# Column steps run one pair ahead with half blocks of gw2 between them, and x's normal form made a second time on GpSimd

## The chip, the cores and the metric

The kernel runs on one core of a Trainium2 chip. The metric is the time of the whole program on the device in microseconds (us); smaller is better. The profile names the engines PE (TensorE, matrix products), PEld (its weight loads), DVE (VectorE), ACT (ScalarE), POOL (GpSimd) and SP (SyncE, which here only issues transfers).

## The reference

One block of a network, forward and backward, in one program. With x of 2048 tokens and 448 channels, and LN a layer norm without weights:

```
h   = x + irfft2( rfft2(LN(x)) * (w_r + i w_i) )
u   = gelu( LN(h)^T w1 + b1 )            # mixes the 2048 tokens into 1792
out = h + ( u w2 + b2 )^T
```

The outputs are `out` and the gradients of x, w_r, w_i, w1, b1, w2 and b2 for a given gradient of `out`; inputs and outputs are bf16. `out_1` is the gradient of x, `out_2` and `out_3` those of w_r and w_i, `out_4` that of w1 (2048x1792), `out_6` that of w2 (1792x2048).

## The kernel before

Tokens lie on the 128 partitions in 16 tiles (`NT`), channels along the row. The program runs in stages, and a scheduler puts the instructions of each engine in one fixed order when the program is built; each engine's queue, and each queue of transfers, is then worked through in that order. `tc.issue_after` and `tc.high_priority` steer it.

1. **Rows forward.** `load_x` brings x in four groups of four tiles. `Norm.stats` and `Norm.finish` make mean and deviation of each group (`nb` is -mean/deviation) and the normal form `xln`; `fft_rows` transforms the rows of a group. Products `dg(j)` of the gradient with w2 (14 of them, 16 matmuls each, L535) fill TensorE meanwhile. Their weights `w2T` come by transposing transfers on SP's queue into a ring of four buffers.
2. **Columns forward.** `fft_cols` makes 9 column steps for r = 0, 8, 1, ..., 7. In a step, `part` runs 8 small matmuls into one or two PSUM tiles, ACT copies one of them (`gi`), DVE adds and subtracts (`gg`), and `out_r` runs three matmuls with `gg` and lets ACT copy the result to `dst`. `cmul` multiplies by the complex filter in six groups of r, `ifft_cols` goes back.
3. SP's queue is a hand-made chain (`nxt`). Behind the tables it holds four stores of `xln` to DRAM (`xln_d`, 448 KB each), then more of `w2T`, `xs_d` (a copy of the spectrum) and `w1c`, the weights of stage 4.
4. **Rows back, MLP forward, and du.** `rows_mid`/`rows_out`, the second norm, gelu (L622), the second product (L691) and `du` times w1 (L748).
5. **Backward block.** The gradient `dh` goes through the same `fft_rows`, `fft_cols`, `cmul` and `ifft_cols` (here with `twice=True`), then `rows_mid_twice` and `rows_out` for each of 16 tiles h. Between them lie the big products: `gw2(j)`, j = 0 to 13, a block of four PSUM tiles of 128x512 (L224: full matmuls, L231: the last 64 rows, two at a time) that four copies empty and one store writes to `out_6`; and `gw1(h)`, 16 blocks, for `out_4`. `outer` issues a block: the full matmuls of its first two tiles, the 64-row ends of all four, the full ones of the last two. Blocks 1 to 5 of `gw2` stand after the column steps in the text, with lower priority, and the scheduler draws their matmuls forward into TensorE's gaps; blocks 6 to 13 follow with h = 0 to 7, then `gw1` with h = 8 to 15, and the last eight blocks of `gw1` in pairs. In the row loop, `norm_back` needs the normal form of x again: `xr`, four tiles at a time in a ring of two buffers, loaded from `xln_d` on POOL's queue. From h = 10 on, `grad_w` makes one of six groups of the gradients of w_r and w_i on DVE from `xs_b`, which is loaded from `xs_d` at h = 7 into the slot that `goT` leaves after the last `gw2`.

Of the kernel before, what the change touches and what calls it, by code (L numbers as in the profile page):

```python
# [135 lines left out]
def kernel(  # L136
# [78 lines left out]
        with tc.issue_after(behind.ins):  # L215
            ld(t[0:64, 3, :], t[64:128, 3, :])

    def outer(first, second, lhs, rhs, shared=True):


        def full(outs, opens):
            for ps, a, b in outs:
                for c in range(3):
                    last = pe.matmul(ps, lhsT=lhs[:, c, a], rhs=rhs[:, c, b],  # L224
                                     start=opens and c == 0, stop=not opens and c == 2)
            return last

        def tails(outs, opens):
            for i, (ps, a, b) in enumerate(outs):
                k = slice(64 * (i % 2), 64 * (i % 2) + 64)  # L230
                last = pe.matmul(ps, lhsT=lhs[k, 3, a], rhs=rhs[k, 3, b], start=opens, stop=not opens)  # L231
            return last

        last = full(first, True)
        with tc.high_priority() if shared else nullcontext(), tc.issue_after(last.ins):
            tails(first, False)
            last = tails(second, True)
        with tc.issue_after(last.ins):
            return full(second, False)

    def ev(out, in_, on):
        if on == "a":
# [62 lines left out]
    gb1 = consts.tile([P, NFB], F32, name="gb1")  # L305
    gb2 = consts.tile([P, NT], F32, name="gb2")

    xln_d = dram.tile([P, NT, D], BF16, name="xln_d")
    xs_d = dram.tile([P, 2, XW], BF16, name="xs_d")
    hn_d = dram.tile([S, D], BF16, name="hn_d")  # L310
    hln_d = dram.tile([NT, P, D], BF16, name="hln_d")
# [4 lines left out]
    class Norm:  # L316
        def __init__(self, src, dst, rstd, eps_col, scale, nm):
            self.src, self.dst, self.rstd, self.eps_col, self.scale, self.nm = src, dst, rstd, eps_col, scale, nm

        def stats(self, h):  # L320
            if h % 4 == 0:
# [8 lines left out]
        def finish(self, g):  # L330
            mv = self.mv[:, :].rearrange("p (i c) -> p i c", c=2)
            r = self.rstd[:, 4 * g:4 * g + 4]
            sq = col(4, f"sq_{self.nm}")
            ac.activation(out=sq[:], in_=mv[:, :, 1], func=ACT.Sqrt, bias=self.eps_col[:], scale=self.scale)
            ve.reciprocal(out=r, in_=sq[:])
            nb = col(4, f"nb_{self.nm}")
            ve.scalar_tensor_tensor(out=nb[:], in0=mv[:, :, 0], scalar=-1.0, in1=r, op0=ALU.mult, op1=ALU.mult)
            for i in range(4):
                h = 4 * g + i

                if (i > 1 or g == 3) if self.nm == "x" else (i > 1 and g == 3):
                    ve.tensor_scalar(out=self.dst[:, h, :], in0=self.src[:, h, :], scalar1=self.rstd[:, h:h + 1],
                                     scalar2=nb[:, i:i + 1], op0=ALU.mult, op1=ALU.add)
                else:
                    ac.activation(out=self.dst[:, h, :], in_=self.src[:, h, :], func=ACT.Identity,  # L345
                                  scale=self.rstd[:, h:h + 1], bias=nb[:, i:i + 1])
# [30 lines left out]
            done = ev(zt[:, :, :, 8 * h:8 * h + 8], pz[:, :, :].rearrange("p c (s k) -> p c s k", k=8), on[i])  # L377
        return last, done

    def fft_cols(zt, dtab, dst, second=None, twice=False):  # L380
        w = 226 if twice else DF

        def part(out, r, odd, s=0):

            if twice:
                for c, chunk in enumerate((3, 2) if odd else (0, 1)):
                    o = 113 * ((2 + 2 * s if odd else 0) + c)
                    pe.matmul(out[:, 113 * c:113 * c + 113], lhsT=zt[:, chunk, r, :], rhs=dtab[:, o:o + 113],
                              start=True, stop=True)
                return  # L390
            for c in range(2):
                o = DF * (2 + 2 * c + s if odd else c)
                pe.matmul(out, lhsT=zt[:, 2 * odd + c, r, :], rhs=dtab[:, o:o + DF], start=(c == 0), stop=(c == 1))

        def sums(nm):
            gg = k1([P, 2, w], nm)
            return gg, gg[:].rearrange("p a (k c) -> p a c k", c=2) if twice else gg[:]

        def by_k(ps):
            return ps[:].rearrange("p a (c k) -> p a c k", c=2) if twice else ps[:]  # L400

        def out_r(r, gg):
            px = ps_sp([P, 2, DF])
            k, i = R_ORDER.index(r) // 8, R_ORDER.index(r) % 8
            pe.matmul(px[:, :, :], lhsT=hf[:, k, 0, i, :], rhs=gg[:, :, 0:DF], start=True, stop=False)  # L405
            pe.matmul(px[:, 0, :], lhsT=hf[:, k, 1, i, :], rhs=gg[:, 1, 0:DF], start=False, stop=False)
            pe.matmul(px[:, 1, :], lhsT=hf[:, k, 2, i, :], rhs=gg[:, 0, 0:DF], start=False, stop=True)
            ac.copy(out=dst[:, :, r * DF:(r + 1) * DF], in_=px[:])

        for r in (0, 8, 1, 2, 3, 4, 5, 6, 7):  # L410
            pr = ps_sp([P, 2, w])
            part(pr[:, 0, :], r, 0)
            part(pr[:, 1, :], r, 1, 0)
            if r in (0, 8):
                gg, out = sums("gg")
                ac.copy(out=out, in_=by_k(pr))
                out_r(r, gg)
                continue
            pi = ps_sp([P, 2, w])
            part(pi[:, 0, :], 16 - r, 1, 1)  # L420
            part(pi[:, 1, :], 16 - r, 0)
            gi = f2([P, 2, w], "gi")
            ac.copy(out=gi[:], in_=pi[:])  # L423
            for rr, op in ((r, ALU.add), (16 - r, ALU.subtract)):
                gg, out = sums("gg")
                last = ve.tensor_tensor(out=out, in0=by_k(pr), in1=by_k(gi), op=op)  # L426
                out_r(rr, gg)
            if r == 2 and second is not None:
                second(last)


    R_GROUPS = ((0, 3), (14, 16), (3, 6), (11, 14), (6, 8), (8, 11))
# [14 lines left out]
                done(r0, r1, last)  # L447


    def ifft_cols(ys, ab, twice=False):  # L450
        lasts = []

        def half(r):
# [14 lines left out]
        for r in (1, 2, 3, 4, 5, 6, 7, 0, 8):  # L468
            p0 = half(r)
            if r in (0, 8):  # L470
                for kind in range(2):
                    ev(ab[:, kind, :, :, r, :], view(p0)[:, kind], "av"[kind])
                continue
            p1 = half(16 - r)
            t1 = f2([P, 2, 2, P], "t1")
            ac.copy(out=t1[:], in_=p1[:])
            st_ = 16 - 2 * r
            ve.tensor_tensor(out=ab[:, 0, :, :, r:17 - r:st_, :].rearrange("p c h k l -> p k c h l"),
                             in0=view(p0), in1=view(t1), op=ALU.add)
            ve.tensor_tensor(out=ab[:, 1, :, :, 16 - r:r - 1:-st_, :].rearrange(  # L480
                "p c h k l -> p k c h l"), in0=view(p0), in1=view(t1), op=ALU.subtract)
# [68 lines left out]
    di0 = table([P, 4 * DF], "di0", "di")  # L550
    kinv = table([P, 3, P], "kinv")
    ident = table([P, P], "ident")
    for g in range(4):
        nxt(ld, xln_d[:, 4 * g:4 * g + 4, :], xln[:, 4 * g:4 * g + 4, :])
    with tc.issue_after(folded[3][1].ins):
        neg(hf[:, 0, 2], hf[:, 0, 1])
    xs = slot(3, [P, 2, XW], "xs")
# [36 lines left out]
    for j in range(4, NFB):  # L594
        dg(j)
        if j == 6:
            nxt(ld, xs_d[:], xs[:])
        if j in (5, 9, 13):
            load_w1c(nxt)


# [155 lines left out]
        load_w(w_b[:, :, 0:XW], lambda load, out, in_: load(out, in_))  # L757
    fft_rows(dh, zt2, 2, "aava", None, True)

    first = []  # L760

    def gw2(j, on):
        s6 = w4([P, S], "s6")
        pws = [ps_mm([P, 512]) for n in range(4)]
        outs = [(pws[n][:], slice(j * P, (j + 1) * P), slice(512 * n, 512 * n + 512)) for n in range(4)]
        mm = outer(outs[:2], outs[2:], g_t, goT)
        for n in range(4):
            ev(s6[:, 512 * n:512 * n + 512], pws[n][:], on[n])
        first.append(mm)
        return st(out_6[j * P:(j + 1) * P, :], s6[:])  # L770

    gw2(0, "aaaa")
    fft_rows(dh, zt2, 3, "aava", first[0], True)
    ds = slot(3, [P, 2, XW], "ds")
    fft_cols(zt2, df0, ds, None, True)
    cmul(lambda r0, r1: (w_b[:, 0, r0 * DF:r1 * DF], w_b[:, 1, r0 * DF:r1 * DF]), ds, w_b, True)
    ab2 = slot(7, [P, 2, 2, NT, NR, 8], "ab2")
    ifft_cols(w_b, ab2, True)

    def small_out(dst, src, n):  # L780
        sb = consts.tile([P, n], BF16, name=f"sb{n}")
# [14 lines left out]
    ld_t4(du_t[:], du_d[:])  # L796
    ld_twice(hlnT, w1T_last)
    ld_twice(du_t, w1T_last)
    xs_b = slot(4, [P, 2, XW], "xs_b")

    def gw1(h, ps):
        s4 = w4([P, F], "s4")
# [14 lines left out]

    def gw1_four(h):
        outs, out = gw1(h, ps_mm)
        outer(outs[:2], outs[2:], hlnT, du_t)  # L820
        out()


    def grad_w(group):
# [11 lines left out]

    for j in range(1, 6):
        gw2(j, "aaaa")  # L840
    mids = [rows_mid_twice(ab2, di1, h) for h in range(2)]
    for h in range(NT):
        if h + 2 < NT:
            mids.append(rows_mid_twice(ab2, di1, h + 2))
        if h % 4 == 0:
            xr = ring.tile([P, 4, D], BF16, tag="xr", bufs=2, name="xr")
            ld(xr[:], xln_d[:, h:h + 4, :], po)
        with tc.issue_after(mids[-1][1].ins):
            py = rows_out(mids[h][0])
        gx = k1([P, D], "gx")  # L850
        norm_back(py, False, xr[:, h % 4, :], rstd_x[:, h:h + 1], -1.0 / D, dh[:, h, :], gx[:])
        st(rows(out_1[0])[:, h, :], gx[:])
        if h < 8:
            gw2(h + 6, "aaav")
        else:
            gw1_four(h - 8)
        if h == 7:
            ld(xs_b[:], xs_d[:])
        if h > 9:
            grad_w(R_GROUPS[h - 10])  # L860

    for h in range(8, NT, 2):
        outs, out = gw1(h, ps_mm)
        outs_2, out_2nd = gw1(h + 1, ps_sp)
        outer(outs, outs_2, hlnT, du_t, False)
# [32 lines left out]
```

## Time and profile before

| | us |
|---|---|
| median of 3 runs (360.67 to 362.02) | 361.34 |
| the profiled execution | 361.35 |
| its span from first to last instruction | 359.5 |

The 1.85 us between the last two lie around the span. The profile page gives busy times by engine and by slices of the span; other views of the same trace list who waited for whom, the chain of work that ended last, the instructions in order of time, and busy time in chosen stretches. A matmul's row is longer than the time that it holds the engine, since matmuls are pipelined and their ends modelled. The granted TensorE clock was 0.997 of full speed over the span.

### The profile page before, as it was taken

The numbers are of one execution on the slowest core, as the hardware profiler recorded it, in microseconds if no ns is written. First come the engines' busy times: TensorE is split into PE (matmuls) and PEld (weight loads), VectorE is DVE, ScalarE is ACT, GpSimd is POOL, SyncE is SP. The second block draws the span as 40 slices with busy tenths as digits, with TensorE's granted clock in tenths as the row PEclk, the third lists the DMA queues.
The fourth block names the chain that finished last, engine by engine and source line by source line (L and its number), as shares of the span: only waits on it lengthen the run. The fifth ranks groups of instructions, "written<-read, shape, count | busy, mean of one in ns | idle before, by whom it ended". The sixth has DMA issues, their size and how long they took to land.

```text
span 359.5 us, 5818 instructions
## 1 busy us (share of the span) xinstructions
PE 334.7 (93%) x2100; PEld 184.9 (51%) x2115; DVE 243.9 (68%) x580; ACT 210.5 (59%) x429; POOL 58.1 (16%) x106
## 2 busy tenths in 40 slices
PE   0799996999999999999999999989999999999994
PEld 0456664666664555555555555544555545454442
DVE  4883776967773999822226887837799997599600
ACT  2574653446658999304703344678766666677573
POOL 1000010001113011330160000010100243335620
PEclk9999999999999999999999999999999999999998
DMA  8999999999699999999999888599293365956664
GB/s 280 265 230 335 241 282 279 283 259 299 206 332 263 320 330 261 319 354 312 214 241 217 173 181 164 201 213 200 89 250 99 142 234 188 352 195 249 239 255 154
DMA packets 132988, 87.18 MB, mean 243 GB/s; under 512 B 92032, under 2 KB 124032, under 8 KB 132576
## 3 DMA queue, kind: packets, MB, share of 16 engines
q1 hardware_dynamic: 124768, 56.48, 65.8%
q0 software_dynamic: 8048, 30.31, 23.4%
q8 instruction: 16, 0.26, 0.3%
q14 instruction: 12, 0.10, 0.1%
q10 hardware_dynamic: 144, 0.03, 0.0%
HBM read 32.52 MB, written 30.76 MB: 176 GB/s over the span
## 4 chain that ended last, share of the span: by engine, by line
PE 71%; DVE 12%; ACT 7%; DMA 7%; issue 2%; ACTq 0%; DVEq 0%
PE ps_mm L224 13%; PE ps_mm L748 12%; PE ps_mm L622 6%; PE ps_sp L691 6%; PE ps_mm L691 6%; DMA w2T<-in_B_w_dram 6%; PE ps_mm L535 6%; PE ps_sp L622 5%; PE ps_mm L231 3%; PE ps_sp L224 2%; ACT s L243 2%; DVE bs_x L324 1%; PE ps_sp L405 1%; ACT zt L243 1%; PE ps_sp L376 1%
## 5 line engine op out<-in xcount | busy, mean ns | idle before, releaser
L243 ACT CAST s<-ps_mm 128x512 bf16<-128x512 f32 x96 | 48.4, 568 | 20.1 <-PE ps_mm L231 13.1
L535 PE MATMUL ps_mm<-go_nat,w2T 128*128 128x448 bf16 x224 | 50.9, 361 | 4.1 <-DMA w2T<-in_B_w_dram 4.1
L748 PE MATMUL ps_mm<-du,w1T 128*128 128x449 bf16 x224 | 43.4, 353 | 0.0
L224 PE MATMUL ps_mm<-goT,g_t 128*128 128x512 bf16 x158 | 41.2, 379 | 0.6 <-issue 0.3
L691 PEld LDWEIGHTS <-w2c 128*128 128x128 bf16 x224 | 21.9, 98 | 20.5
L748 PEld LDWEIGHTS <-w1T 128*128 128x128 bf16 x224 | 21.7, 97 | 20.7
L622 PEld LDWEIGHTS <-w1c 128*128 128x128 bf16 x224 | 21.8, 98 | 19.9 <-issue 1.0
L535 PEld LDWEIGHTS <-w2T 128*128 128x128 bf16 x224 | 21.8, 99 | 20.0 <-DMA w2T<-in_B_w_dram 5.4
L691 PE MATMUL ps_sp<-gT,w2c 128*128 128x448 bf16 x112 | 30.3, 352 | 0.0
L691 PE MATMUL ps_mm<-gT,w2c 128*128 128x448 bf16 x112 | 30.3, 352 | 0.0
L224 PE MATMUL ps_mm<-du_t,hlnT 128*128 128x512 bf16 (+1 forms) x141 | 30.1, 352 | 0.3 <-issue 0.2
L224 PEld LDWEIGHTS <-hlnT 128*128 128x128 bf16 x192 | 17.8, 98 | 20.5 <-issue 5.1
L426 DVE TENSOR_TENSOR gg<-ps_sp,gi 128x450 bf16<-128x450 f32 (+1 forms) x28 | 16.6, 642 | 16.8 <-ACT gi L423 16.8
L194 POOL DMA_DIRECT2D out_dram<-s x29 | 15.6, 538 | 62.6 <-ACT s L243 51.3
L622 PE MATMUL ps_mm<-hln,w1c 128*128 128x448 bf16 x112 | 23.8, 352 | 0.3 <-ACT hln L345 0.3
L712 ACT ACTIVATE nm<-ps_mm,rstd_h 128x1 f32<-128x1 f32 x16 | 4.2, 262 | 33.8 <-PE ps_mm L748 33.8
L224 PEld LDWEIGHTS <-g_t 128*128 128x128 bf16 x168 | 15.1, 97 | 15.5 <-issue 3.9
L622 PE MATMUL ps_sp<-hln,w1c 128*128 128x448 bf16 x112 | 22.8, 352 | 0.0
L696 DVE SCALAR_TENSOR_TENSOR h<-ps_mm,b2col,hr 128x448 bf16<-128x448 f32 x8 | 5.1, 680 | 25.8 <-PE ps_mm L691 25.8
L703 ACT ACTIVATE junk<-go_r 128x448 bf16<-128x448 bf16 x16 | 9.2, 576 | 18.4 <-DMA go_r<-in_grad_out_dram 18.0
L243 ACT CAST zt<-ps_sp 128x512 bf16<-128x512 f32 x26 | 13.4, 596 | 6.9 <-PE ps_sp L376 6.9
L578 DVE TENSOR_TENSOR x<-ps_sp,x 128x448 bf16<-128x448 f32 x16 | 10.0, 625 | 9.5 <-PE ps_sp L515 8.6
(157 smaller groups left out, 661.5 us busy)
## 6 DMA issues: line engine op xcount, KB each, us to landing
w1c<-in_B_w_dram SPq DMA_DIRECT2D x7, 1024.0 KB, 7.0
w2c<-in_B_w_dram SPq DMA_DIRECT2D x8, 896.0 KB, 12.4
out_dram<-s POOLq DMA_DIRECT2D x14, 512.0 KB, 3.0
out_dram<-s POOLq DMA_DIRECT2D x15, 448.0 KB, 3.0
xs_d<-xs SPq DMA_DIRECT2D x1, 1800.0 KB, 7.4
xs_b<-xs_d SPq DMA_DIRECT2D x1, 1800.0 KB, 9.9
x<-in_A_x_dram SPq DMA_DIRECT2D x4, 448.0 KB, 4.3
go_nat<-in_grad_out_dram SPq DMA_DIRECT2D x2, 896.0 KB, 7.3
```

Source lines behind the costliest of these rows:

```text
L194: return (eng or po).dma_start(out=out, in_=in_)
L224: last = pe.matmul(ps, lhsT=lhs[:, c, a], rhs=rhs[:, c, b], start=opens and c == 0, stop=not opens and c == 2)
L231: last = pe.matmul(ps, lhsT=lhs[k, 3, a], rhs=rhs[k, 3, b], start=opens, stop=not opens)
L243: return ac.copy(out=out, in_=in_)
L426: last = ve.tensor_tensor(out=out, in0=by_k(pr), in1=by_k(gi), op=op)
L535: pe.matmul(pg[:], lhsT=w2T[j][:, t, :], rhs=go_nat[:, t, :], start=(t == 0), stop=(t == NT - 1))
L578: ve.tensor_tensor(out=hn[:, h, :], in0=py[:], in1=x[:, h, :], op=ALU.add)
L622: pe.matmul(pu[:], lhsT=wc[:, h, o:o + P], rhs=hln[:, h, :], start=(h == 0), stop=(h == NT - 1))
L691: pe.matmul(p2[i][:], lhsT=w2c[t0 // 4][:, j, i * P:(i + 1) * P], rhs=gT[:, j, :], start=(j == 0), stop=(j == NFB - 1))
L696: ve.scalar_tensor_tensor(out=h2[:], in0=p2[i][:], scalar=b2col[:, t:t + 1], in1=hr[:, i, :], op0=ALU.add, op1=ALU.add)
L703: ac.activation(out=junk[:], in_=go_r[:, h, :], func=ACT.Copy, accum_out=gb2[:, h:h + 1])
L748: w1_last = pe.matmul(pd[:], lhsT=w1T[:, j, :], rhs=du[:, j, 0:D + 1], start=(j == 0), stop=(j == NFB - 1))
```

## The change

Three things change. (1) `outer` becomes the generator `halves`, which stops after each half block; the blocks of `gw2` from 1 and of `gw1` stand in one queue, `blocks()`, and `fill(n)` takes n halves from it: one or two in each backward column step, one at r = 1, 3, 5 of the backward `ifft_cols`, two (one block) in each step of the row loop. In the backward column steps `out_r` of one pair of r is issued behind `part` of the next pair. In the row loop `gw2` so ends at h = 5 and not 7, `xs_b` is loaded at h = 5, `grad_w` runs at h = 8 to 13, ten blocks of `gw1` lie in the loop and six behind it. (2) The four stores of `xln_d` are gone. `xr` is loaded from x itself, again on POOL's queue, and GpSimd makes the normal form of each tile in place with one `tensor_scalar` (16 in all); `nb` is kept in a tile of its own. (3) The loads of `w1c` stand behind `dg(7)`, `dg(10)` and `dg(13)`, not 5, 9 and 13.

In the order that the scheduler makes of it, POOL's queue issues the first two loads of `xr` right behind the two small loads of `b1r` and `b2r` at the start, since nothing holds them any more, and the first eight `tensor_scalar` stand behind them; the other eight lie between the stores of the row loop. The ninth `w2T` (for `dg(8)`) stands on SP's queue right behind the tables, followed by two more, `xs_d`, another `w2T`, and then the first `w1c`.

```
-    def outer(first, second, lhs, rhs, shared=True):
+    def halves(first, second, lhs, rhs, shared=True):
...
             tails(first, False)
             last = tails(second, True)
+        yield last
         with tc.issue_after(last.ins):
-            return full(second, False)
+            last = full(second, False)
+        yield last
+
+    def outer(*args):
+        return list(halves(*args))[-1]
...
-    xln_d = dram.tile([P, NT, D], BF16, name="xln_d")
...
+            self.nb = consts.tile([P, NT], F32, name=f"nb_{nm}")
...
-    def fft_cols(zt, dtab, dst, second=None, twice=False):
+    def fft_cols(zt, dtab, dst, second=None, twice=False, fill=None):
...
+        waiting = []
         for r in (0, 8, 1, 2, 3, 4, 5, 6, 7):
             pr = ps_sp([P, 2, w])
             part(pr[:, 0, :], r, 0)
             part(pr[:, 1, :], r, 1, 0)
+            done = []
             if r in (0, 8):
                 gg, out = sums("gg")
                 ac.copy(out=out, in_=by_k(pr))
-                out_r(r, gg)
-                continue
...
+                done.append((r, gg))
+            else:
+                pi = ps_sp([P, 2, w])
+                part(pi[:, 0, :], 16 - r, 1, 1)
+                part(pi[:, 1, :], 16 - r, 0)
+                gi = f2([P, 2, w], "gi")
+                ac.copy(out=gi[:], in_=pi[:])
+                for rr, op in ((r, ALU.add), (16 - r, ALU.subtract)):
+                    gg, out = sums("gg")
+                    last = ve.tensor_tensor(out=out, in0=by_k(pr), in1=by_k(gi), op=op)
+                    done.append((rr, gg))
...
+            waiting += done
+            if not fill or r:
+                for rr, gg in waiting if not fill else waiting[:-len(done)]:
+                    out_r(rr, gg)
+                waiting = done if fill else []
+                if fill:
+                    fill(2 if r in (3, 6) else 1)
+        for rr, gg in waiting:
+            out_r(rr, gg)
...
             p1 = half(16 - r)
+            if fill and r in (1, 3, 5):
+                fill(1)
...
-    for g in range(4):
-        nxt(ld, xln_d[:, 4 * g:4 * g + 4, :], xln[:, 4 * g:4 * g + 4, :])
...
-        if j in (5, 9, 13):
+        if j in (7, 10, 13):
             load_w1c(nxt)
...
-        mm = outer(outs[:2], outs[2:], g_t, goT)
-        for n in range(4):
-            ev(s6[:, 512 * n:512 * n + 512], pws[n][:], on[n])
...
+        for i, mm in enumerate(halves(outs[:2], outs[2:], g_t, goT)):
+            for n in (2 * i, 2 * i + 1):
+                ev(s6[:, 512 * n:512 * n + 512], pws[n][:], on[n])
+            if i:
+                st(out_6[j * P:(j + 1) * P, :], s6[:])
+            yield mm
...
+    def blocks():
+        for j in range(1, NFB):
+            yield from gw2(j, "aaaa" if j < 7 else "aaav")
+        for h in range(NT):
+            yield from gw1_four(h)
+
+    others = blocks()
+
+    def fill(n):
+        return [next(others) for i in range(n)]
+
     ds = slot(3, [P, 2, XW], "ds")
-    fft_cols(zt2, df0, ds, None, True)
+    fill(1)
+    fft_cols(zt2, df0, ds, None, True, fill)
...
-    ifft_cols(w_b, ab2, True)
+    ifft_cols(w_b, ab2, True, fill)
...
-    for j in range(1, 6):
-        gw2(j, "aaaa")
...
-            ld(xr[:], xln_d[:, h:h + 4, :], po)
+            ld(xr[:], rows(A_x[0])[:, h:h + 4, :], po)
+
+            for i in range(h, h + 4):
+                po.tensor_scalar(out=xr[:, i - h, :], in0=xr[:, i - h, :], scalar1=rstd_x[:, i:i + 1],
+                                 scalar2=nx.nb[:, i:i + 1], op0=ALU.mult, op1=ALU.add)
...
-        if h < 8:
-            gw2(h + 6, "aaav")
-        else:
-            gw1_four(h - 8)
-        if h == 7:
+        fill(2)
+        if h == 5:
+            xs_b = slot(4, [P, 2, XW], "xs_b")
             ld(xs_b[:], xs_d[:])
-        if h > 9:
-            grad_w(R_GROUPS[h - 10])
-
-    for h in range(8, NT, 2):
+        if 8 <= h < 14:
+            grad_w(R_GROUPS[h - 8])
+
+    for h in range(10, NT, 2):
```

More of the change, by code (lines that the diff above doesn't have):

```diff
@@ L335, in finish @@
             ve.reciprocal(out=r, in_=sq[:])
-            nb = col(4, f"nb_{self.nm}")
-            ve.scalar_tensor_tensor(out=nb[:], in0=mv[:, :, 0], scalar=-1.0, in1=r, op0=ALU.mult, op1=ALU.mult)
+            nb = self.nb[:, 4 * g:4 * g + 4]
+            ve.scalar_tensor_tensor(out=nb, in0=mv[:, :, 0], scalar=-1.0, in1=r, op0=ALU.mult, op1=ALU.mult)
             for i in range(4):
@@ L416, in fft_cols @@
                 ac.copy(out=out, in_=by_k(pr))
-                out_r(r, gg)
-                continue
[L419 to L429, printed above, removed]
+                done.append((r, gg))
[9 more added lines that the diff above has]
+                    done.append((rr, gg))
+                if r == 2 and second is not None:
+                    second(last)
+            waiting += done
[7 more added lines that the diff above has]
+            out_r(rr, gg)
     R_GROUPS = ((0, 3), (14, 16), (3, 6), (11, 14), (6, 8), (8, 11))
@@ L447, in cmul, with ifft_cols @@
                 done(r0, r1, last)
-    def ifft_cols(ys, ab, twice=False):
+    def ifft_cols(ys, ab, twice=False, fill=None):
         lasts = []
@@ L758 @@
     fft_rows(dh, zt2, 2, "aava", None, True)
-    first = []
     def gw2(j, on):
@@ L765, in gw2 @@
         outs = [(pws[n][:], slice(j * P, (j + 1) * P), slice(512 * n, 512 * n + 512)) for n in range(4)]
-        mm = outer(outs[:2], outs[2:], g_t, goT)
-        for n in range(4):
-            ev(s6[:, 512 * n:512 * n + 512], pws[n][:], on[n])
[L769 to L773, printed above, removed]
+        for i, mm in enumerate(halves(outs[:2], outs[2:], g_t, goT)):
[4 more added lines that the diff above has]
+            yield mm
+    first = list(gw2(0, "aaaa"))
+    fft_rows(dh, zt2, 3, "aava", first[-1], True)
+    def blocks():
[6 more added lines that the diff above has]
+        return [next(others) for i in range(n)]
     ds = slot(3, [P, 2, XW], "ds")
-    fft_cols(zt2, df0, ds, None, True)
+    fill(1)
+    fft_cols(zt2, df0, ds, None, True, fill)
     cmul(lambda r0, r1: (w_b[:, 0, r0 * DF:r1 * DF], w_b[:, 1, r0 * DF:r1 * DF]), ds, w_b, True)
     ab2 = slot(7, [P, 2, 2, NT, NR, 8], "ab2")
-    ifft_cols(w_b, ab2, True)
+    ifft_cols(w_b, ab2, True, fill)
     def small_out(dst, src, n):
@@ L798 @@
     ld_twice(du_t, w1T_last)
-    xs_b = slot(4, [P, 2, XW], "xs_b")
     def gw1(h, ps):
@@ L819, in gw1_four @@
         outs, out = gw1(h, ps_mm)
-        outer(outs[:2], outs[2:], hlnT, du_t)
-        out()
+        for i, mm in enumerate(halves(outs[:2], outs[2:], hlnT, du_t)):
+            if i:
+                out()
+            yield mm
     def grad_w(group):
```

## The prediction

> **What bounds the kernel now.** The page first, then TensorE's waits over the whole run, then the chain that ended last.
>
> ```profile
> span 359.5 us, 5818 instructions
> PE 334.7 (93%) x2100; PEld 184.9 (51%) x2115; DVE 243.9 (68%) x580; ACT 210.5 (59%) x429; POOL 58.1 (16%) x106
> DMA  8999999999699999999999888599293365956664
> ```
>
> TensorE is busy for 93% of the span, so a change can only win idle time of TensorE or its late start and end. The transfer engines are nearly full in the first 27 of 40 slices, up to some 240 us. So a transfer that is moved into that part pushes others back.
>
> ```profile
> PE ps_sp L376 <- DVE eo L370: 10.9, 1, 10.9
> PE ps_mm L535 <- DMA w2T<-in_B_w_dram: 4.1, 2, 3.5
> PE ps_sp L405 <- DVE gg L426: 1.2, 5, 0.4
> PE ps_sp L405 <- ACT gg L416: 0.5, 1, 0.5
> ...
> 47.45 11.25 DMA w2T<-in_B_w_dram
> ...
> 289.98 1.29 PE ps_mm L224 x6
> ...
> 352.93 2.24 ACT s L243 x5
> ```
>
> The first four lines are waits (total us, times, longest), the others stand in the chain (start, us, what). TensorE starts at 10.9, when the first rows are ready. It then stands still once for long, 3.5 us before `dg(8)`, because its weights `w2T` come late, and 0.6 us before `dg(11)`. In the backward column steps it waits for `gg` of DVE and ACT, 1.7 us as shown. At the end nothing is hidden: the last copies take 2.24 us and their stores the rest. Six matmuls of 512 columns take 1.29 us, 0.215 each.
>
> **The change part by part.** The sum is made against the profiled execution: 361.35 us, span 359.5 and 1.85 around it. It is 0.01 off the median of the runs shown, 361.34.
>
> *The start.* The loads of `xr` wait for nothing now, and two of them move to the head of POOL's queue.
>
> ```profile
> 0.74 0.39 SPq L191 DMA_DIRECT2D x<-in_A_x_dram  x1
> ...
> 1.92 0.54 POOL L191 DMA_DIRECT2D b2r<-in_B_b_dram  x1
> 2.27 0.71 SPq L191 DMA_DIRECT2D go_nat<-in_grad_out_dram  x1
> ...
> 3.02 7.61 SPq L197 DMA_TRANSPOSE w2T<-in_B_w_dram  x1
> ...
> 8.73 0.62 DVE L324 BATCH_NORM_STATS2 bs_x<-x 128x6 f32<-128x448 bf16 x1
> ...
> 10.69 1.04 SPq L191 DMA_DIRECT2D x<-in_A_x_dram  x2
> ...
> 10.88 1.89 PE L376 MATMUL ps_sp<-kf,eo 128*128 128x128 bf16 x16 [10.88 <-DVE eo L370]
> ...
> 12.74 1.68 PE L535 MATMUL ps_mm<-go_nat,w2T 128*128 128x448 bf16 x4
> ...
> 5.00:10.00 5.00, 0.00 (x0) 0.00 (x0) 4.36 (x14) 1.71 (x3) 0.00 (x0) 1.00 1.13 379
> 10.00:15.00 5.00, 4.12 (x23) 2.56 (x24) 3.87 (x15) 3.04 (x7) 0.00 (x0) 1.00 1.08 268
> ...
> go_nat<-in_grad_out_dram SPq DMA_DIRECT2D x2, 896.0 KB, 7.3
> xln_d<-xln SPq DMA_DIRECT2D x4, 448.0 KB, 8.4
> xr<-xln_d POOLq DMA_DIRECT2D x4, 448.0 KB, 5.8
> ```
>
> SP's queue issues x, go_nat, x, go_nat and then the first `w2T`, whose row ends at 10.63 and holds up the next loads of x until 10.69. I read that as: it waits until the loads ahead have landed. POOL would issue its two loads from 2.5 us on (1.92 + 0.54), when only the first x is about done. They are 2 x 448 KB, 0.92 MB, and the stretch from 5 to 10 us moves 379 GB/s at a full share (1.13): 2.4 us of transfer ahead of everything that is still queued. Second group of x: 896 KB before 10.63, so landed at about 8.2, used by DVE at 8.73 in front of `eo`. It would land at 10.6, so DVE and the first matmul are 1.9 later; `w2T`, and `dg(0)` at 12.74, 2.4 later. I take +2.1. Bounds: 0, if POOL's loads only fill gaps, and 3.4, at the 268 GB/s of the stretch behind.
>
> The Trainium skill, "Trainium Kernel Development and Optimization", section Key Constraints, says that transfers from the SP, ACT and POOL queues run on the same 16 engines and interleave, which speaks against this part of the change; that the share exceeds 1 here fits it.
>
> *The wait for w2T.* The four stores of `xln`, 1.8 MB, stood ahead of the ninth `w2T`, and the early `xr` loads from them ran beside it.
>
> ```profile
> SPq L197 <- DMA hi<-tab_hi: 1.8, 1, 1.8
> ...
> L191 SPq DMA_DIRECT2D xln_d<-xln x4: 366/540/1040, 42.8 to 44.6; - x4
> ...
> 78.88 0.74 PE ps_mm L535 x3
> ...
> 95.03 1.05 PE ps_mm L622 x5
> ...
> w1c<-in_B_w_dram SPq DMA_DIRECT2D x7, 1024.0 KB, 7.0
> ...
> ident<-tab_ident SPq DMA_DIRECT2D x1, 32.0 KB, 7.7
> ...
> 56.68 0.69 DVE L247 TENSOR_SCALAR hi<-hi 128x2048 bf16<-128x2048 bf16 x1
> ...
> 58.74 0.55 PE L535 MATMUL ps_mm<-go_nat,w2T 128*128 128x448 bf16 x2 [3.54 <-DMA w2T<-in_B_w_dram]
> ```
>
> In the new order that `w2T` stands where the first store stood, right behind the tables; it no longer waits for `hi`. Before, it was issued at 47.45 and landed 11.25 later. Issued where the first store was, at 42.8, behind `ident` (landed 7.7 after an issue just before that, so by 50), and given the 4 to 5 us that are left of the 11.25 without the stores, it lands at about 54, or 56 with the late start. `dg(8)` wants it at 55.2 (58.74 less 3.54), or 57.3 with the late start. So the wait goes: 3.54 shown, and 0.16 more, because a 512-column matmul's row is 0.378 long where the next starts after 0.215. What is late next is DVE, busy to 57.4 (56.68 + 0.69) with the filter, which TensorE's pause had hidden: up to 0.8. I take -3.4, between -3.7 and -2.9. The 0.6 before `dg(11)` goes too: the first two loads of `w1c`, 2 MB, no longer stand ahead of `xs_d` and that `w2T` (bounds 0 and -0.8). Moving `w1c` costs nothing as long as it lands before L622 starts, at 95; it now stands behind the `w2T` that `dg(11)` uses at 78.9. If it were late, `dg(12)` would wait for it first.
>
> *GpSimd's 16 pieces.* No row shows such an operation on GpSimd. The nearest are the same operation on DVE and ACT:
>
> ```profile
> L342 DVE TENSOR_SCALAR xln<-x,rstd_x,nb_x x10: 379/392/398, 8.1 to 24.6; 128x448 bf16<-128x448 bf16 x10
> L345 ACT ACTIVATE xln<-x,nb_x,rstd_x x6: 744/754/760, 8.1 to 21.4; 128x448 bf16<-128x448 bf16 x6
> ```
>
> 0.39 to 0.75, and I take 0.75, the slower engine's. Queued behind them are stores on POOL, which have no reader but the ring of four buffers. They delay nobody unless they slow DVE (a rival, below). For that I put +0.2 at the start.
>
> *Column steps.* The half blocks now fill what DVE and ACT leave.
>
> ```profile
> 236.00:264.00 28.00, 25.82 (x198) 13.71 (x200) 17.52 (x31) 23.47 (x46) 2.67 (x5) 1.00 0.82 176
> 264.00:282.00 18.00, 17.50 (x132) 11.24 (x132) 16.60 (x35) 11.34 (x24) 1.07 (x2) 1.00 0.60 157
> 282.00:335.00 53.00, 52.35 (x332) 25.38 (x337) 45.90 (x112) 35.80 (x78) 20.27 (x38) 1.00 0.62 229
> ...
> L224 PE MATMUL ps_mm<-goT,g_t 128*128 128x512 bf16 x49 | 13.0, 378 | 0.2 <-issue 0.2
> L243 ACT CAST s<-ps_mm 128x512 bf16<-128x512 f32 x19 | 10.7, 595 | 2.5 <-PE ps_mm L231 2.2
> ...
> L405 PE MATMUL ps_sp<-gg,hf 128*128 128x450 bf16 x16 | 5.7, 354 | 1.7 <-DVE gg L426 1.0 <-ACT gg L416 0.5
> ...
> DVE t_r L441 <- DMA xs_b<-xs_d: 3.2, 1, 3.2
> ```
>
> (Stretches: length, then busy PE, PEld, DVE, ACT, POOL, clock, DMA; then groups of 236 to 264.) In the steps from 236 to 264 TensorE waits for DVE's `gg` 1.0 shown, four times, each 0.16 more: 1.6. A pair of lead covers that, since DVE then has a half block (6 x 0.215) and the other pair's `out_r` to finish. The wait for ACT at r = 0 and 8 stays. But ACT is at 23.5 of 28, and the new order puts about one block more into this stage: four copies of 0.595, 2.4, so 25.9 in 26.4. `gi` then stands behind copies. And `ifft_cols` behind it (264 to 282) has DVE at 16.6 of 18, whatever TensorE does. I take -0.9, bounds -1.6 and +0.6 (one copy late on the chain).
>
> *The row loop.* TensorE's work is the same, 52.35 of 53. `xs_b` comes two steps earlier, and so does DVE's 3.2 wait for it; five and not three groups of `grad_w` stand ahead of the last `eo`. Cover: `rows_mid_twice` runs two steps ahead, and DVE has 53 - 45.9 - 3.2 = 3.9 left. The last eight pieces of GpSimd fall here. I take +0.2, bounds 0 and 3.0 (four pieces of 0.75 where DVE is full). The end is the same, three pairs of `gw1` and not four.
>
> Sum: +2.1 - 3.4 - 0.6 + 0.2 - 0.9 + 0.2 = -2.4, so 361.35 - 2.4 = 359.0 us. A measurement can tell about 0.5% from no change: 1.8 us, below 359.5 or above 363.2.
>
> **The rivals.** *The start costs nothing.* POOL's loads run in gaps, or land after the second x. For it: the slice before 5 us is not full. Against: the share of 1.13 from 5 on. Then 359.0 - 2.1 = 356.9.
>
> *Slower: GpSimd and DVE block each other.* If a piece on GpSimd holds up a DVE operation with two inputs in memory for its length, the four `eo` operations of the first two groups, on the chain to the first matmuls, lose up to 4 x 0.75 = 3.0. In the row loop, where `grad_w` fills DVE, four pieces cost 3.0 less about 1.0 of lead: 2.0. With 5.0 in place of the 0.4: 359.0 + 4.6 = 363.6. It makes the kernel slower once the eight collisions cost more than 2.8 together, 0.35 each. For it: DVE is nearly full in both places. Against: many pieces meet one-input operations, or a DVE that waits. The page "SBUF — State Buffer" of the Trainium skill, section Who interferes with whom, states that rule: a GpSimd instruction that reads this memory and a DVE one with two inputs there lock each other out for the whole instruction. No run here shows it yet, since POOL only issued transfers.
>
> *The column steps give nothing.* ACT is the limit at 98%, and DVE's backlog eats 0.5 of the `w2T` wait: +2.1 - 2.9 - 0.6 + 0.6 + 0.4 = -0.4, so 360.9.
>
> **How the numbers follow.** My forecast 0.43, own range 357.7 to 360.3; the free start 0.18; collisions 0.17; column steps without gain 0.22. Faster by over 0.5%: six tenths of the first (0.27), nearly all of the second (0.17), a little of the last: 0.46. Slower: most of the collisions, and some 0.03 for what I do not see: 0.13. Same: 0.41. The range 356.2 to 363.0 holds the forecast, the last rival, most of the second and a part of the collisions.
>
> **What would show it.** Right: the first matmul (10.88) near 12.9 and `dg(0)` near 15; no wait of L535 for `w2T` over 0.5; L405 waiting for DVE under 0.5 in all; pieces of `xr` on POOL of 0.4 to 0.8; DVE's wait for `xs_b` unchanged near 3. Wrong: a first matmul still at 10.9; `eo` rows of L365 longer than 0.63 at the start, or DVE rows in the row loop longer than now, with TensorE waiting for `eo`; a new wait of L405 or of the ifft for ACT; or a `w2T` that is late again, behind `xs_d`.

## The result, and the profile after

The changed kernel takes 357.89 us (median of 6 runs, 357.04 to 358.67); the kernel before took 361.68 beside it (6 runs). The ratio, a figure of its own and not the quotient of these medians, is 0.9876, with a 95% interval from 0.9840 to 0.9912. Run once more in a later comparison, unedited, it took 357.63 at a ratio of 0.9873 (0.9837 to 0.9909). So it is faster by 1.2 to 1.3%, or 4.5 us by the ratio (the medians differ by 3.8 here and by 4.8 in the repeat), where 359.0 and a gain of 2.4 were forecast; the time lies in the range. Medians and ratios leave out slow executions, over 1.5% above the fastest of the same kernel: below, one of e1, one of e10 and one of the kernel before.

The page of the profiled execution (358.53 us), span and engines:

```profile
span 356.7 us, 5854 instructions
PE 335.2 (94%) x2115; PEld 185.4 (52%) x2115; DVE 246.6 (69%) x579; ACT 209.6 (59%) x430; POOL 72.8 (20%) x122
```

POOL has 14.7 us more to do, the 16 pieces; TensorE's 15 more records are records that the trace of before lacked (its weight loads were 2115 there too). TensorE's rows in order of time, with the matmuls that answer to 10.88, 12.74 and 95.0 of before:

```profile
12.06 1.89 PE L381 MATMUL ps_sp<-kf,eo 128*128 128x128 bf16 x16 [12.06 <-DVE eo L375]
15.23 5.02 PE L555 MATMUL ps_mm<-go_nat,w2T 128*128 128x448 bf16 x14 [1.28 <-DMA w2T<-in_B_w_dram]
...
41.52 1.50 PE L555 MATMUL ps_mm<-go_nat,w2T 128*128 128x448 bf16 x7 [1.07 <-DMA w2T<-in_B_w_dram]
...
94.97 1.12 PE L640 MATMUL ps_mm<-hln,w1c 128*128 128x448 bf16 x5
```

The start is later, as forecast, `w2T` is waited for at new places (before `dg(0)` and, at 41.5, before `dg(5)`), and the first gelu matmul stands at 94.97, where it stood before. By this profile alone the front half nets nothing, and nearly the whole gain of 2.8 in the span (2.55 of it) comes from the backward block. The second profile of the same kernel says otherwise (356.69 us, span 354.8):

```profile
11.04 1.89 PE L381 MATMUL ps_sp<-kf,eo 128*128 128x128 bf16 x16 [11.04 <-DVE eo L375]
14.33 4.79 PE L555 MATMUL ps_mm<-go_nat,w2T 128*128 128x448 bf16 x15 [1.40 <-DMA w2T<-in_B_w_dram]
...
39.62 1.50 PE L555 MATMUL ps_mm<-go_nat,w2T 128*128 128x448 bf16 x7 [0.50 <-DMA w2T<-in_B_w_dram]
...
93.09 1.12 PE L640 MATMUL ps_mm<-hln,w1c 128*128 128x448 bf16 x5
```

There the first gelu matmul is 1.9 earlier than before. The start is full of transfers, and they land at different times in two executions of one program: the first `w2T` at 15.19 and 14.29, and the one for `dg(5)` is waited for 1.07 and 0.50. Together these are 1.5 of the 1.9.

The backward block is the same in both. Its stretches (length, then busy PE, PEld, DVE, ACT, POOL, clock, DMA share, GB/s) are: the column steps; `cmul` and `ifft_cols`; the row loop; the last blocks. First before, then after:

```profile
237.84:263.86 26.02, 24.07 (x175) 12.71 (x180) 16.69 (x30) 21.71 (x43) 2.13 (x4) 1.00 0.78 167
263.86:277.32 13.46, 13.16 (x93) 8.38 (x93) 13.46 (x26) 7.78 (x16) 0.53 (x1) 1.00 0.72 174
277.32:328.89 51.57, 50.72 (x334) 25.40 (x341) 43.07 (x108) 36.36 (x79) 18.09 (x34) 1.00 0.58 213
328.89:354.74 25.85, 25.64 (x148) 12.16 (x147) 9.86 (x22) 16.75 (x38) 10.35 (x20) 1.00 0.63 237
```
```profile
237.84:263.85 26.01, 25.70 (x192) 13.90 (x192) 17.15 (x30) 21.43 (x45) 2.67 (x5) 1.00 0.87 172
263.85:277.55 13.70, 13.43 (x95) 8.59 (x94) 13.19 (x24) 8.63 (x17) 1.06 (x2) 1.00 0.99 243
277.55:331.94 54.39, 54.24 (x360) 26.74 (x360) 47.99 (x117) 38.65 (x84) 28.82 (x47) 1.00 0.60 218
331.94:352.18 20.24, 20.24 (x118) 9.47 (x115) 6.57 (x16) 13.17 (x30) 7.17 (x14) 1.00 0.55 211
```

The lengths alone mislead: the column steps take 26.0 us in both. But 12 more weight loads (180 to 192) went by in them, so 12 more matmuls lie there, three quarters of a block of 16; the row loop has 19 more and the end 32 fewer. The four stretches sum to 116.90 before and 114.34 after. That is where 2.56 us come from.

### The profile page after: what moved, and what is told of

It reads as the page before. It is cut to its first block, busy times and chain, and to the rows that moved or that the text cites. A ratio compares the mean times of both kernels' runs of the same rounds, so it can differ in the third digit from the quotient of the medians.

```text
span 356.7 us, 5854 instructions
## 1 busy us (share of the span) xinstructions
PE 335.2 (94%) x2115; PEld 185.4 (52%) x2115; DVE 246.6 (69%) x579; ACT 209.6 (59%) x430; POOL 72.8 (20%) x122
## 4 chain that ended last, share of the span: by engine, by line
PE 80%; DMA 7%; DVE 5%; ACT 5%; issue 1%; SPq 1%; ACTq 0%
PE ps_mm L224 17%; PE ps_mm L766 12%; PE ps_mm L555 8%; DMA w2T<-in_B_w_dram 7%; PE ps_mm L640 6%; PE ps_sp L709 6%; PE ps_mm L709 6%; PE ps_sp L640 5%; PE ps_mm L231 3%; PE ps_sp L477 2%; PE ps_sp L410 2%; PE ps_sp L224 1%; PE ps_sp L478 1%; ACT s L248 1%; ACT zt L248 1%; PE ps_sp L532 1%
## 5 line engine op out<-in xcount | busy, mean ns | idle before, releaser
L248 ACT CAST s<-ps_mm 128x512 bf16<-128x512 f32 (+1 forms) x101 | 50.6, 568 | 22.9 <-PE ps_mm L231 18.3
L224 PE MATMUL ps_mm<-goT,g_t 128*128 128x512 bf16 x168 | 42.0, 380 | 0.0
L224 PE MATMUL ps_mm<-du_t,hlnT 128*128 128x512 bf16 (+1 forms) x156 | 33.2, 353 | 0.0
L879 POOL TENSOR_SCALAR xr<-xr,rstd_x,nb_x 128x448 bf16<-128x448 bf16 x16 | 14.7, 923 | 15.4 <-DMA xr<-in_A_x_dram 13.1
```

The source lines that it names most:

```text
L224: last = pe.matmul(ps, lhsT=lhs[:, c, a], rhs=rhs[:, c, b], start=opens and c == 0, stop=not opens and c == 2)
L248: return ac.copy(out=out, in_=in_)
L879: po.tensor_scalar(out=xr[:, i - h, :], in0=xr[:, i - h, :], scalar1=rstd_x[:, i:i + 1], scalar2=nx.nb[:, i:i + 1], op0=ALU.mult, op1=ALU.add)
```

## The experiments

The first explanation was: the half blocks and the lead bring the whole gain, and the front nets nothing, because the two early loads of `xr` cost what the dropped `xln_d` stores give. The rivals: the cost at the start is GpSimd's pieces, not the transfers; or the columns give nothing and the gain is the front's.

The table gives, for each profile, the start of the first matmul, of `dg(0)`, of the first gelu matmul and of the last matmul of du, and the time from the start of the first column part to the start of the last matmul of a gradient block ("backward"); then the median of the runs and the ratio to the kernel before. The kernel before took 362.5 in each of the three comparisons (e1 to e4, e5 to e8, e9 to e11); a profile is one execution, the median is over 5 to 12 runs.

| kernel | first | dg(0) | gelu | du | backward | median | ratio (95%) |
|---|---|---|---|---|---|---|---|
| before | 10.88 | 12.74 | 94.97 | 229.74 | 116.69 | | 1 |
| after | 12.06 | 15.23 | 94.97 | 229.73 | 114.13 | 357.89 | 0.9876 (0.9840 to 0.9912) |
| after again (e11) | 11.04 | 14.33 | 93.09 | 227.84 | 114.14 | 357.63 | 0.9873 (0.9837 to 0.9909) |
| loads held to 184 us (e1) | 10.68 | 12.57 | 90.94 | 230.46 | 114.52 | 357.11 | 0.9880 (0.9827 to 0.9932) |
| pieces alone held (e2) | 11.03 | 14.47 | 92.54 | 227.29 | 114.22 | 357.55 | 0.9868 (0.9839 to 0.9896) |
| first half alone (e3) | 10.59 | 12.54 | 95.34 | 230.10 | 114.14 | 359.81 | 0.9932 (0.9906 to 0.9958) |
| second half alone (e4) | 11.38 | 14.60 | 92.98 | 229.78 | 117.85 | 360.59 | 0.9955 (0.9926 to 0.9984) |
| loads held to 231 us (e5) | 10.31 | 12.46 | 90.14 | 224.90 | 115.36 | 356.35 | 0.9821 (0.9788 to 0.9855) |
| e5, w1c at 5, 9, 13 (e6) | 10.58 | 12.75 | 91.19 | 225.95 | 115.49 | 356.30 | 0.9828 (0.9793 to 0.9863) |
| half blocks, no lead (e7) | 10.45 | 12.33 | 94.42 | 229.18 | 116.46 | 361.96 | 1.0000 (0.9965 to 1.0035) |
| lead, whole blocks (e8) | 10.66 | 12.52 | 97.96 | 232.73 | 114.80 | 360.47 | 0.9959 (0.9927 to 0.9991) |
| loads held to the first MLP product (e9) | 10.53 | 12.52 | 90.82 | 226.44 | 114.59 | 355.35 | 0.9808 (0.9770 to 0.9846) |
| one load held (e10) | 11.13 | 13.66 | 91.80 | 226.55 | 114.90 | 356.21 | 0.9841 (0.9798 to 0.9885) |

**The two halves apart.** e3 takes the first half alone; its edits, against the changed kernel, put the stores and the old source of `xr` back:

```
+    for g in range(4):
+        nxt(ld, xln_d[:, 4 * g:4 * g + 4, :], xln[:, 4 * g:4 * g + 4, :])
...
-            ld(xr[:], rows(A_x[0])[:, h:h + 4, :], po)
+            ld(xr[:], xln_d[:, h:h + 4, :], po)
...
-        if j in (7, 10, 13):
+        if j in (5, 9, 13):
```

(and the pieces go). e4 makes the opposite edits, and the pieces, in the kernel before.

> The first half of the change alone: half blocks of gw2 in fixed places and column steps one pair ahead, xs_b from h = 5, grad_w from h = 8; xln_d is stored as before, xr comes from it, w1c goes out at j = 5, 9, 13 as before. Theory 'the whole gain is in the backward block': front as before (dg(0) 12.7, dg(8) 58.7), end of the GELU and MLP stages as before, 2.4 to 3.3 us gained behind 240 us (more than the 2.6 of the changed kernel if its row loop loses to GpSimd's pieces): 361.5 minus 2.9 = 358.2 to 359.1. Rival 'columns give nothing' (my prediction's case of 360.9): 361 to 361.7, and the gain is the front's.

> The second half of the change alone: no xln_d, the normal form made again by GpSimd from x, w1c at j = 7, 10, 13; the backward block is that of the kernel before, whole blocks and no lead. Theory 'the whole gain is in the backward block': dg(0) 15.2, dg(8) 59.3, first GELU block where the kernel before has it; the row loop loses 0 to 1 to the pieces: 361.4 to 362.5. Rival 'columns give nothing': 357.9 to 359.

The first half gives 0.68%, 2.5 us, and its backward block is that of the changed kernel (114.14). "Columns give nothing" falls. But the second half alone gives 0.45%, 1.6 us, so "the whole gain is in the backward block" falls too. The two add up to 4.1 of the 4.5 that both give together. In e4's profile the front is 2.0 ahead at the first gelu matmul, and has lost it at the end of du. That execution took 362.52, the slowest of its 12, and shows where:

```profile
PE ps_mm L746 <- DMA w1T<-in_B_w_dram: 1.7, 2, 1.2
...
172.81 15.39 SPq L197 DMA_TRANSPOSE goT<-in_grad_out_dram  x2
188.29 14.04 SPq L197 DMA_TRANSPOSE w1T<-in_B_w_dram  x5
```

The two transposing loads of `goT` held SP's queue for 15.4 us, in the repeat e11 for 12.1; the loads of `w1T`, the weights of du, stand behind them, and TensorE, which comes earlier now, waits for them.

**What costs the start: transfers or pieces.** e1 holds the first two loads and the eight pieces behind the last store of `out_0`, e2 the pieces alone:

```
+            with tc.issue_after(h2_last.ins):       # e1 alone
                 ld(xr[:], rows(A_x[0])[:, h:h + 4, :], po)
             for i in range(h, h + 4):
+                with tc.issue_after(h2_last.ins):
                     po.tensor_scalar(...)
```

> The changed kernel, with the first two loads of xr and their eight GpSimd pieces put on GpSimd's queue behind the last store of out_0 (near 200 us) instead of at its head. Theory 'early loads' (the front nets nothing because these two transfers at 2.45 and 3.02 us push x, go_nat and the first w2T back): first matmul from 12.06 back to 10.9, dg(0) from 15.23 to 12.7, the new 1.2 us wait for w2T before dg(5) gone, dg(8) from 59.28 to 55.8 to 56.8, dg(11) 2.5 to 3.1 earlier; in all 2.5 to 3.1 us off the changed kernel's 357.9, so 354.8 to 355.4. Rival 'something later holds the front anyway' (w2T, w1c or hln): dg(0) comes earlier, the first GELU block does not, and the time stays within 0.5 of 357.9. Rival 'ports': as the first, since the pieces go as well.

> The changed kernel, with the two early loads of xr left at the head and only their eight GpSimd pieces held behind the last store of out_0. Theory 'early loads': dg(0) stays at 14.9 to 15.3 and the w2T wait before dg(5) stays; the three slow VectorE operations (969, 971 and 720 ns for 627, 620 and 395) become quick, which is worth 0 to 0.5 us, so 357.4 to 357.9. Theory 'ports' (the pieces on the port that VectorE shares cost the start): dg(0) back to 13.2 or earlier and 2 to 3 us gained, 355 to 356.

With the pieces gone from the start and the loads left, `dg(0)` is still late (14.47; with the pieces 14.33, 14.60 and 15.23) and the time is the same within the intervals. With the loads gone too it is at 12.57. So the transfers cost the start (the eight profiles without early loads have `dg(0)` at 12.33 to 12.75, the four with two at 14.33 to 15.23), and the pieces nothing that can be measured. The size of e1's gain was a miss, though: 4.0 at the first gelu matmul, more than expected, and then all of it lost again in du in the profiled execution.

```profile
PE ps_mm L766 <- DMA w1T<-in_B_w_dram: 3.2, 1, 3.2
...
184.05 18.26 SPq L197 DMA_TRANSPOSE w1T<-in_B_w_dram  x5
184.09 1.07 POOL L191 DMA_DIRECT2D xr<-in_A_x_dram  x2
...
185.00:215.00 30.00, 26.82 (x145) 13.58 (x144) 22.46 (x50) 9.98 (x22) 8.25 (x9) 0.94 1.06 183
```

The held loads were issued 0.04 us behind the first of the five `w1T` loads, and TensorE waited 3.2 for one of these; a lower clock in that stretch of this execution (0.94) did the rest. The cause was then put so: two loads of 448 KB cost about 2 us wherever a transposing load is waited for. That is not shown: of e1's six executions, three took 355.7 to 357.1 us at a clock of 0.997 and more, as quick as e5, e6 and e9 below, and three 359.7 to 362.8 at 0.995, the profiled one among them. So the loss in du is not in all of them, and load and clock were not taken apart.

**Where the loads may stand.** e5 holds them (and with them the pieces) behind the first store of `out_6`, e9 behind the last store of `hln_d`; e6 is e5 with `w1c` at j = 5, 9, 13; e10 is e9 with the load of h = 0 left at the head.

```
+            with tc.issue_after(stores[0].ins):     # e5, e6; hln_last.ins in e9, in e10 for h > 0
                 ld(xr[:], rows(A_x[0])[:, h:h + 4, :], po)
```

> The changed kernel, with the first two loads of xr and their eight GpSimd pieces behind the store of the first gw2 block (near 235 us), where no transposing load waits. Theory 'slack' (the two loads cost the start 2 us wherever x and w2T wait, and cost again when they are held only to 184 us, because the w1T loads, behind goT on SP's queue, have some 2 us to spare there): dg(0) 12.6, first GELU block near 91.0 (before 95.0), last matmul of du near 225.7 to 226.7 (before 229.7) with waits for w1T under 1, then the backward block as in the changed kernel: 2 to 4 us less than the changed kernel's profile, 352.5 to 354.5 in the span, 354 to 356 in the median. Rival 'w1T is late whatever comes earlier': first GELU block near 91, but du ends at 229 or later again, and the time is that of the changed kernel (357.9).

> As the run before it, with w1c's loads at j = 5, 9, 13 again instead of 7, 10, 13. Theory 'stores' (w2T came late because the four xln_d stores and their reads stood ahead of it): no wait for w2T over 0.5 before dg(8), time within 0.5 of the run before it. Rival 'w1c' (it was the moved load of w1c that freed w2T): a wait for w2T of 2 to 3.5 before dg(8) or dg(9), first GELU block at 93.5 to 94.5, 2 to 3 us slower than the run before it unless w1T takes it back.

> The changed kernel, with the first two loads of xr and their eight GpSimd pieces behind the last store of hln_d (near 95 us), in the stage of the first MLP product, where TensorE waits for nothing. Theory 'early loads, then slack, then ports': dg(0) 12.5, first GELU block 90 to 91, end of du 225 to 226 as with the loads near 235 us; and the stretch from the first column part to the last gw matmul, which was 115.4 and 115.5 with the pieces beside the column steps, back to the 114.1 of the changed kernel: span 351.5 to 352.8, median 354.5 to 355.5. Rival 'no free place': the two loads delay w1c or w2c there and TensorE waits 1 to 4 us in the first MLP product; span 353 or more.

> As the run before it, but the load of xr for h = 0 with its four pieces stays at the head of GpSimd's queue, and only that of h = 4 goes behind the last store of hln_d. Theory 'transfers share the start': half the price, dg(0) at 13.3 to 14.0 instead of 12.5 (two early loads: 14.5 to 15.2). Rival 'one queue slot' (it is the second of the two, or that a load stands there at all): dg(0) at 12.5 or at 14.5 and later.

> The changed kernel once more, unedited. What the start and the w1T stage cost in another execution: dg(0) 14.4 to 15.3, the wait for w2T before dg(5) 1 to 2, first GELU block between 92.5 (as with the pieces held) and 95.0 (as in its first profile); the stretch from the first column part to the last gw matmul 114.1. Theory 'the front nets nothing': first GELU block at 95, end of du at 229.7. Theory 'the front nets 2, when w1T is not late': 92.5 to 93.2 and 227.2 to 227.8.

One early load puts `dg(0)` in the middle:

```profile
12.52 3.77 PE L555 MATMUL ps_mm<-go_nat,w2T 128*128 128x448 bf16 x15
```
```profile
13.66 3.73 PE L555 MATMUL ps_mm<-go_nat,w2T 128*128 128x448 bf16 x15 [0.65 <-DMA w2T<-in_B_w_dram]
```

(e9 with none, e10 with one; with two, 14.33 to 15.23.) So 1.1 us for one load of 448 KB, from one profile each, and 1.8 to 2.7 for two. Without early loads the front keeps its gain: 4.8 in e5 up to the end of du. In e9, whose held loads go out at 114 us, 3.3 of 4.2 are left there, with 0.5 of shown waits for `w1T` between, so `w1T` can be late without them beside it. The rival "w1T is late whatever comes earlier" falls, and so does "no free place". e6 has no `w2T` wait over 0.5 and e5's time, so moving `w1c` neither gave nor cost: the gone stores freed `w2T`, together with the two early reads of `xln_d` behind them, which no run takes apart.

In e5 the pieces lie beside the backward columns. Its column steps and two groups of DVE there, against e9's column steps:

```profile
233.00:259.49 26.49, 25.93 (x191) 13.88 (x192) 17.86 (x30) 21.90 (x46) 10.52 (x13) 1.00 1.04 186
...
L459 DVE TENSOR_TENSOR t_r<-ds,w_b 128x1350 bf16<-128x1350 bf16 x4 | 3.7, 932 | 0.0
...
L461 DVE TENSOR_TENSOR w_b<-t_r,t_i 128x675 bf16<-128x675 bf16 x4 | 2.4, 588 | 0.0
```
```profile
234.54:260.56 26.02, 25.70 (x191) 13.90 (x192) 17.15 (x30) 21.44 (x45) 2.67 (x5) 1.00 0.79 168
```

The two groups of `cmul` take 932 and 588 ns on average for 850 and 499 in e9, the column steps 0.47 longer. The backward block is 0.8 longer than e9's; most of the rest is in the row loop (55.21 for 54.84), where TensorE waits 0.7 for a copy of ACT, and not beside these pieces. e9's block is at 114.59, not at the 114.1 expected; 0.45 of that is in the row loop, with 0.3 of it a wait for a copy of ACT, and the rest was not traced. e9 has the lowest median: 355.35 us, 2.3 below the changed kernel beside it (357.63), and five of its six executions lie below all six of that. Against the kernel before its ratio is 0.9808, the intervals of the two just overlap. The runs do not separate it from e5 and e6 (0.9821 and 0.9828).

**Lead and half blocks apart.** e7 is e3 without the lead:

```
-            waiting += done
-            ...
+            for rr, gg in done:
+                out_r(rr, gg)
+            if fill and r:
+                fill(2 if r in (3, 6) else 1)
```

e8 is the kernel before with the lead alone (`waiting` as in the change, no `fill`; the scheduler places whole blocks).

> The first half of the change without the lead: half blocks of gw2 in the same fixed places, out_r of a pair directly behind that pair's parts; xln_d stored as before. Theory 'the lead counts': PE waits for VectorE's gg sums again at the column steps (1.0 us in 4 waits before), the half block between two pairs hides part of them; the stretch from the first part to the last gw matmul (116.7 before, 114.1 with the lead) is 114.5 to 115.5. Theory 'the fixed half blocks alone': 114.0 to 114.4, as with the lead.

> The kernel before, with the column steps one pair ahead and nothing else: whole blocks of gw2 where the scheduler puts them, xln_d, xs_b and grad_w as before. Theory 'the fixed half blocks count' (17 more recorded gw2 matmuls done before the row loop, where PE was idle): the stretch from the first part to the last gw matmul stays at 116.2 to 116.8. Theory 'the lead counts': 115.5 or less, the waits for gg at the column steps under 0.5.

The backward block is 116.69 without both, 116.46 with the half blocks, 114.80 with the lead, 114.13 with both. The lead carries it. (e7's 116.46 is longer than either theory gave it, 114.0 to 115.5, and its time is that of the kernel before.) e7's column steps, TensorE's waits for `gg` in the backward block of e7, and its one for `gg` in e8:

```profile
237.28:265.66 28.38, 26.85 (x192) 13.60 (x193) 17.43 (x30) 22.66 (x45) 2.67 (x5) 1.00 0.75 148
...
PE ps_sp L411 <- DVE gg L435: 1.1, 4, 0.4
PE ps_sp L411 <- ACT gg L425: 0.3, 1, 0.3
```
```profile
PE ps_sp L405 <- ACT gg L418: 0.3, 1, 0.3
```

Half blocks in fixed places leave the four waits for DVE as they were (1.0 before); the lead takes them away. With the same half blocks in them, the column steps take 28.38 without the lead and 26.01 with it. e8's front is 3 us late in its profile (a clock of 0.94 from 60 to 100 us), which its backward block does not show.

## Why the prediction was right, point by point

The sum said -2.4, and by the ratio 4.5 was gained; the front was to give 1.7 of it and gave about 2, the backward block 0.7 and gave 2.55. So the time fell into the range though one term was far too small. The terms are these.

*The start, +2.1: right in kind and size.* `dg(0)` is 1.6 and 2.5 later in the two profiles, `dg(1)` 2.1 and 3.2. The path is the forecast one: the second go_nat lands at 12.47 and 13.37 (10.83 before) and the first `w2T` 1.8 to 1.9 behind it, as before. The first matmul was forecast near 12.9 and came at 12.06 and 11.04: the second x lands 0.7 and 1.5 late (9.07 and 9.83, 8.34 before), not 2.4, and the first `w2T` carries the delay. That SP and POOL share the engines, which the Trainium skill, "Trainium Kernel Development and Optimization", section Key Constraints, states, agrees with e9 and e10: a load on POOL's queue put back one on SP's by 1.1.

*The waits for w2T, -3.4 and -0.6: right.* With no early load, where nothing else moves the front, the first gelu matmul is 3.8 to 4.8 earlier (e1, e5, e6, e9), for 4.0. Together with the start the front was to give 1.7 with GpSimd's 0.2, and gave 0.0, 1.9, 2.0 (e4) and 2.4 (e2). "No wait for `w2T` over 0.5" was wrong: waits of 1.28 and 1.40 stand before `dg(0)`, and new ones of 1.07 and 0.50 before `dg(5)`. The step that was not seen is that of e1 and e4: what the front gains, `w1T` can take back at du.

*The column steps, -0.9: the term that was mis-sized.* The backward block, for which the sum had -0.9 and +0.2, measured -2.55. The step that failed is the limit: ACT was taken to be full after the change, at 25.9 of 26.4. Weight loads of the blocks in this stretch before, then groups of it after:

```profile
L224 PEld LDWEIGHTS <-g_t 128*128 128x128 bf16 x52 | 4.6, 97 | 3.7 <-issue 0.4
...
L231 PEld LDWEIGHTS <-g_t 64*128 64x128 bf16 x16 | 0.5, 94 | 1.7 <-issue 1.7
```
```profile
L224 PEld LDWEIGHTS <-g_t 128*128 128x128 bf16 x60 | 5.7, 98 | 5.3 <-issue 0.8
...
L231 PEld LDWEIGHTS <-g_t 64*128 64x128 bf16 x20 | 0.6, 94 | 2.1 <-issue 2.1
...
L248 ACT CAST s<-ps_mm 128x512 bf16<-128x512 f32 x22 | 12.2, 602 | 4.6 <-PE ps_mm L231 4.5
L413 ACT CAST ds<-ps_sp 128x450 bf16<-128x450 f32 x14 | 7.2, 575 | 0.0
...
L224 PE MATMUL ps_mm<-goT,g_t 128*128 128x512 bf16 x60 | 14.8, 379 | 0.0
L410 PE MATMUL ps_sp<-gg,hf 128*128 128x450 bf16 x16 | 5.7, 354 | 0.3 <-ACT gg L425 0.3
```

TensorE does eight full matmuls and four 64-row ends more (its weight loads count them; the trace of before lacks four of the matmul records). ACT makes three copies more, and yet is busy for 21.43 of 26.01, where it was 21.71 of 26.02: it stands idle for 4.6 before its copies, waiting for TensorE. A busy time of 23.5 in 28 was read as little room; the same view said that ACT's idle time ended with TensorE. Eight full matmuls at 0.215 and four ends at 0.54 together (both by rows of the chain of before) are some 2.3, and they fit into the same 26.0, so 2.3 of idle time went, where 0.9 was forecast and 1.6 was the bound. 1.6 of it are the waits for DVE as the prediction counted them, 0.2 is ACT's `gg` (0.5 to 0.3), and 0.5 is not read off any wait (the one issue gap that the prediction's row shows, 0.2, may be a missing record). The other 0.3 of the 2.55 went behind the column steps and is not traced to a wait. `ifft_cols`, where DVE was full before (13.46 of 13.46), is 0.24 longer.

*The row loop, +0.2: right for the pieces.* The loop takes 54.39 with the pieces (after, e11) and 54.39 without them (e3). In the old order of that loop e4 takes 52.71 for 51.57, with 0.7 of waits for ACT's copies; DVE also waits 4.6 for `xs_b` there and not 3.2, so how much of it the pieces cost is open. DVE's wait for `xs_b` fell to 1.7, where "near 3" was written.

*The rivals.* The start was not free. The column steps did give something. And the collisions between GpSimd and DVE exist: with the pieces beside them two of DVE's first four operations on `eo` take half as long again (0.62 before):

```profile
L879 POOL TENSOR_SCALAR xr<-xr,rstd_x,nb_x x16: 704/776/1607, 9.6 to 318.0; 128x448 bf16<-128x448 bf16 x16
...
10.94 0.97 DVE L371 TENSOR_TENSOR eo<-xln 128x892 bf16<-128x892 bf16 x1
...
17.90 0.97 DVE L370 TENSOR_TENSOR eo<-xln 128x892 bf16<-128x892 bf16 x1
...
300.21 1.05 DVE L739 TENSOR_TENSOR gx<-junk,go_r 128x448 bf16<-128x448 bf16 x1
```

Each of these two cost 0.35, just the price from which the rival was to decide, but two `eo` operations were hit and not four, and e2 shows that they cost TensorE nothing: it waits for `w2T` at `dg(0)` anyway. A one-input operation was hit as well (one `xln` takes 0.72 for 0.39), where the prediction had counted such operations as safe. In the row loop five rows of DVE are longer by 1.9 together, `gx` (0.39 without a piece) by 0.66 beside a piece of 0.71. That is near the 2.0 of the rival, but TensorE waits for none of it: the loop is as long in e3, without pieces. The rule of the Trainium skill, "SBUF — State Buffer", section Who interferes with whom, agrees in kind.

## What to carry to other kernels

A matmul that waits for a chain of other engines is helped by issuing it one step later, with anything in between: here that gave 1.9 of 2.55 alone, while fixed places for the filling work gave 0.2 alone. An engine that is busy for 84% of a stage (23.5 of 28) is not its limit when its idle time ends with the engine that it should be limiting. And a load that waits for nothing went to the head of its queue here, into a start that is full of transfers: one load of 448 KB put `dg(0)` back by 1.1 us, and both behind a store in the middle of the program gave 2.3 us of the whole time back.

## What the runs showed of the hardware that was not expected

One piece on GpSimd (128x448, bf16, two scalars per partition) takes 0.704 us at the least and up to 1.61 in the changed kernel and 2.69 in e5, where DVE works beside it; DVE's rows are longer there by up to 0.66, so the two delay each other. And two executions of one program differ by 1.9 us at the first gelu matmul (94.97 and 93.09) at a full clock, 1.5 of it where transfers land later: from one profile the front seemed to give nothing, and only a second profile and the halves apart showed that it gives about 2.
